# Key rows and row sums of the first sequence's v by 0/1 matrices on TensorE, loads in the order k and q, v, weights, and conversions of weight sets 2 to 4 queued behind attention unit 3

## The chip, the core and the metric

One Trainium2 chip, of which the kernel uses one core. The metric is the device time of one execution in microseconds (us): 1023.42 us, the median of three runs (1019.8 to 1023.69). Five engines run their own queues in order: TensorE (PE, with its weight loads as PEld), VectorE (DVE), ScalarE (ACT), GpSimd (POOL) and SyncE (SP), which issues all DMAs.

## The reference

The inputs q, k, v are 4 sequences x 8 heads x 576 rows x 64 channels, fp32. Two attentions are added, and two expert layers follow on the 2304 x 512 result:

```python
q_d = q.reshape(B, H, Sd, factor, D).mean(axis=3)     # factor 4: 144 rows; k_d, v_d alike
out_up = np.repeat(sm_attn(q_d, k_d, v_d), factor, axis=2)
mask = np.abs(pos[:, None] - pos[None, :]) < factor    # local attention, 7 keys a row
out = out_up + softmax(scale * q @ k.T where mask) @ v
x = ((g := x @ w_gate) * sigmoid(g) * (x @ w_val)) @ w_out       # 512 -> 1536 -> 512
h = x @ w_in;  x = (max(h, 0) + alpha * min(h, 0)) @ w2_out       # 512 -> 2048 -> 512
```

## The kernel before, in words

Attention goes in units: a unit `n` is two heads and half a sequence (288 rows), four units a half, so units 0 to 7 are the first sequence. A unit transposes q (and, in the first half, k) on TensorE (`a_T`), multiplies them (`a_QK`), takes the two softmaxes (`a_EXP`, `a_NRM`), transposes the weights of the coarse one (`a_PT`) and multiplies both with v (`a_PV`), whose result `xf` is split into a high and a low part, `xh` and `xl`.

`a_PV` needs v in two forms. `vw` holds the key rows in windows: for each 24 queries 32 rows of v, 128 partitions a tile. For it `stage(0)` copies v into a DRAM tensor `vwin` with overlapping windows, and `a_load_w` reads that back. `vs` holds sums of four neighbouring rows: `a_load_v` loads v once more as `vd`, and `a_vd` adds on GpSimd (L321, L322).

The expert layers multiply in three fp32r products of high and low parts. So every weight tile is converted once: `w_split` takes a raw tile through ScalarE (L126), VectorE (L127, L128), ScalarE (L131) and GpSimd (L132). A set j is three tiles, g, v and o, of the first layer (12 sets). The first layer runs over 8 blocks of 288 rows: block 0 is units 0 to 3, and its step j multiplies with tile g (`m_g`, ended by L502), tile v (`m_v`, ended by L508) and, one step later, tile o (`m_y`). During block 0 all 12 sets are loaded and converted. The later units run beside the matmuls.

SBUF is full: attention tiles of units 0 to 7 live in slots of weight tiles that come later (`pslot`). Of the 24 slots of sets 4 to 11, in the order g4 v4 o4 g5, v5 o5 g6 v6, o6 g7 v7 o7, g8 v8 o8 g9, v9 o9 g10 v10, the first four hold `qv` (q and vw of units 0 to 3), the next four `qs` (softmax tiles), then `kn`, `vd` and `bd`. Units 4 to 7 put their `qv` where `kn` was and their `qs` where `vd` was. A weight tile is loaded when the attention tile in its slot has been read for the last time. The converted halves go through three staging tiles in rotation (`st_slots`).

A scheduler orders each engine's queue by a time model of its own; `tc.issue_after` holds an instruction behind a named one. In `prep1` the table `gP` puts GpSimd's part of sets 1, 2 and 3 behind units 0 and 3, the other engines' parts are not held. The loads of unit 8 stand behind the load of tile o7.

Of the kernel before, what the change touches and what calls it, by code (L numbers as in the profile page):

```python
# [15 lines left out]
DRAM = bass.MemoryType.DRAM  # L16


K = dict(kdP=0, qdP=0, dnP=2, ldn=9, lo='asvw0123', NPRO=8, c=5, a1=1, a2=0, OFF=25, oT=3, oE=3, oP=5, oV=11, vd1=2, vd2=1, pre=(1, 1, 0, 0), lo1=0, lo2=1, nst=3, nrm=0, sub=0, nrm1=0, sub1=0, qtA=0, ldw=1, xl1=0, ly=4, l2=3, st2=2, early=1, w2p=1, la=0, bdV=0, sp=9, s2=0, s3=0, gj=7, gs=1, vr=0, kc=0, gD=(0, 0, 0, 0, 0, 0), gP=(0, 2, 8, 8, 0, 0), gA=(0, 0, 0, 0, 0, 0))


@with_exitstack
def attn_moe_moe2_kernel(
# [113 lines left out]
    pbd = {}  # L137
    kds = {}
    vss = {}
    vds = {}  # L140
    bds = [ap_.tile([128, 2, NW, 128], F32, name=f"bd{i}", bufs=1) for i in range(NBD)]

    def coords(n):
# [4 lines left out]
    order = [f"{kind}{j}" for j in range(F1 - 8, F1) for kind in "gvo"]  # L148
    st_slots = order[5 * NP:][:K["nst"]]
    NEARLY = F1 - 2  # L150
    pslot = {(what, n): order[4 * i + n] for i, what in enumerate(("qv", "qs", "kn", "vd", "bd")) for n in range(NP)}
    for n in range(NP):
        pslot["qv", n + NP] = pslot["kn", n]
        pslot["qs", n + NP] = pslot["qs" if K["vr"] else "vd", n]
    NPRO = K["NPRO"]
    srs = [ap_.tile([128, 8], F32, name=f"sr{i}", bufs=1) for i in range(4)]

    def at_(n, shape, tag):
        return wp.tile(shape, F32, tag=pslot[tag, n], name=tag)
# [23 lines left out]
    def a_load(n):  # L183
# [22 lines left out]
        for h in range(2):  # L206
            nc.sync.dma_start(out=qn[:, :, h], in_=q[b, h0 + h, t0:t0 + HB, :].rearrange("(r p) c -> p r c", p=QB))

    def a_load_v(n):
        b, half, hp, blk = coords(n)  # L210
        h0 = 2 * hp
        if half == 0:
            hu[n]["vd"] = []
            if n < NP:
                vd = vds[hp] = at_(n, [72, 2, 2, 4 * D], "vd")
                nc.sync.dma_start(out=vd.rearrange("p h f x -> p (h f) x"),
                                  in_=v[b, h0:h0 + 2].rearrange("h (f p r) c -> p (h f) (r c)", f=2, r=4))
            for f in range(2):
                if n < NP:
                    hu[n]["vd"].append(vd[:, :, f])  # L220
                    continue
                vf = ap_.tile([72, 2, 4 * D], F32, tag="vd", name="vd", bufs=NVD)
                hu[n]["vd"].append(vf)
                nc.sync.dma_start(out=vf, in_=v[b, h0:h0 + 2, f * HB:(f + 1) * HB].rearrange("h (p r) c -> p h (r c)", r=4))

    def a_load_w(n):

        b, half, hp, blk = coords(n)
        if n < NP:
            pbd[n] = at_(n, [128, 2, NW, 128], "bd")  # L230
            (nc.vector if K["bdV"] else nc.gpsimd).memset(pbd[n], 0.0)
        if n >= NPRO:
            hu[n]["vw"] = ap_.tile([128, NW, 2, D], F32, tag="vw", name="vw", bufs=NVW)
        t = hu[n]["vw"]
        for h in range(2):
            w0 = ((b * H + 2 * hp + h) * 2 + half) * NW * 128
            nc.sync.dma_start(out=t[:, :, h], in_=vwin[w0:w0 + NW * 128, :].rearrange("(w p) c -> p w c", p=128))

    def stage(b):

        nw = H * S // SUB
        g0, g1, ng = b * nw, (b + 1) * nw, B * nw

        def win(a, e):
            n = (e - a) * SWIN
            nc.sync.dma_start(
                out=vwin[a * SWIN:e * SWIN, :].rearrange("(g r) c -> g (r c)", r=SWIN),
                in_=bass.AP(v.tensor, v.offset + (a * SUB - 3) * D, [[SUB * D, e - a], [1, SWIN * D]]))

        vf = v.rearrange("b h s c -> (b h s) c")  # L250
        if g0 == 0:
            nc.sync.dma_start(out=vwin[0:3, :], in_=vf[0:3, :])
            nc.sync.dma_start(out=vwin[3:SWIN, :], in_=vf[0:SWIN - 3, :])
            win(1, 16)
            g0 = 16
# [56 lines left out]

    def a_vd(n):
        b, half, hp, blk = coords(n)
        if n < NPRO and K["vr"]:
            return
        if half == 0:
            vs = vss[hp] = ap_.tile([72, 2, 2, D], F32, tag=f"vs{hp}", name="vs", bufs=1)
            for f in range(2):
                vv = hu[n]["vd"][f].rearrange("p h (r c) -> p h r c", r=4)  # L320
                nc.gpsimd.tensor_tensor(out=vv[:, :, 0:2], in0=vv[:, :, 0:2], in1=vv[:, :, 2:4], op=ALU.add)  # L321
                nc.gpsimd.tensor_tensor(out=vs[:, f], in0=vv[:, :, 0], in1=vv[:, :, 1], op=ALU.add)  # L322

    def a_QK(n, A):
        b, half, hp, blk = coords(n)
# [94 lines left out]
    def a_PV(n, A):  # L420
        b, half, hp, blk = coords(n)
        d = hu[n]
        pt, vw, bd = d["pt"], d["vw"], d["bd"]
        if n < NPRO and K["vr"]:
            vd = vds[hp].rearrange("p h f (r c) -> p h f r c", r=4)
            for f in range(2):
                for r in range(4):
                    for h in range(2):
                        nc.tensor.matmul(A[64 * h:64 * h + 64, 1, 0:QD], vd[:, h, f, r], pt[:, h, f * QD:(f + 1) * QD],
                                         start=(f == r == 0), stop=(f == 1 and r == 3))  # L430
        else:
            vs = vss[hp]
            for f in range(2):
                for h in range(2):
                    nc.tensor.matmul(A[64 * h:64 * h + 64, 1, 0:QD], vs[:, f, h], pt[:, h, f * QD:(f + 1) * QD],
                                     start=(f == 0), stop=(f == 1))
# [12 lines left out]
        nc.gpsimd.tensor_sub(xl[:, hp], xf, f32(xh[:, hp]))
        del hu[n]  # L450
# [26 lines left out]
    def gate(n, stage):  # L477

        bb = tc.nc.cur_bb.bb.instructions
        for key, eng in (("D", nc.vector), ("P", nc.gpsimd), ("A", nc.scalar)):  # L480
            gates[key, n, stage] = next(i for i in reversed(bb) if i.engine == eng.engine)

    def prep1(j):
        with ExitStack() as es:
            for key in "DPA":
                g = K["g" + key][j] if j < 6 else 0
                if g and (key, (g - 1) // 2, (g - 1) % 2) in gates:
                    es.enter_context(tc.issue_after(gates[key, (g - 1) // 2, (g - 1) % 2]))
# [129 lines left out]

    if True:
        make_identity(nc, ident)  # L620
        for tok in K["lo"]:
            if tok == "s":
                stage(0)
            elif tok in "avw":
                for n in range(NP):
                    {"a": a_load, "v": a_load_v, "w": a_load_w}[tok](n)
            elif tok == "x":
                for n in range(NP):
                    a_load_v(n)
                    a_load_w(n)  # L630
            else:
                load1(int(tok))
# [20 lines left out]
        P = [ATT, Y[0], Y[1], pgv.tile([128, 2, 512], F32, name="gv")]  # L653
        def a_all(n, A):
            a_T(n, A)
            if K["vd1"] == 0:
                a_vd(n)
            a_QK(n, A)
            gate(n, 0)
            if K["vd1"] == 1:  # L660
                a_vd(n)
            a_EXP(n)
            a_NRM(n)
            gate(n, 1)
# [169 lines left out]
```

## Time and profile before

| what | value |
|---|---|
| median of three runs | 1023.42 us |
| profiled execution, its own time | 1022.0 us |
| its span, first to last instruction | 1020.1 us |
| PE busy | 970.3 us, 95% of the span |
| DVE, POOL, ACT busy | 496.7, 387.7, 292.3 us |
| PE idle in the first 51.73 us | 28.4 us |

The 1.9 us between the span and the profiled time lie around the program and are not touched by the change. In the 40 slices of the profile PE is under 90% busy only in the first six and in the last one, so the time of this kernel beyond its matmuls lies in the first 150 us. There DVE is the busiest engine (5898884 in its first seven slices), and the DMA engines are at eight to nine tenths in the first three.

### The profile page before, as it was taken

How to read it: one execution, taken by the hardware profiler on the slowest of the kernel's cores; microseconds unless marked ns; L12 is line 12 of the kernel's file. 1: busy time of each engine (PE TensorE's matmuls, PEld its weight loads, DVE VectorE, ACT ScalarE, POOL GpSimd, SP SyncE). 2: the span in 40 equal slices, each digit the busy share in tenths (PEclk: the TensorE clock that was granted, in tenths of full speed). 3: DMA queues.
4: the chain of work that ended last, by engine and by line, in shares of the span. 5: the costliest groups of instructions: out<-in, count | busy, mean ns of one | idle time of the engine just before them, and what ended most of it. 6: DMA issues, size and time to landing. Idle time of an engine off the chain costs nothing.

```text
span 1020.1 us, 19253 instructions
## 1 busy us (share of the span) xinstructions
PE 970.3 (95%) x7760; PEld 867.5 (85%) x7760; DVE 496.7 (49%) x1045; ACT 292.3 (29%) x660; POOL 387.7 (38%) x492
## 2 busy tenths in 40 slices
PE   5388789999999999999999999999999999999997
PEld 4288789999999999999999998888888888888896
DVE  5898884546453646353532769722322322322232
ACT  3656542222222222222223656312101101111111
POOL 5868773233422343322223335724223322322222
PEclk9999999999999999999999999999999999999999
DMA  8996751123120232110103884102000100100010
GB/s 199 289 305 217 196 139 39 35 67 60 42 51 16 54 71 45 38 29 15 43 13 88 290 265 127 42 1 62 21 0 19 55 1 1 42 11 0 1 43 21
DMA packets 135895, 77.81 MB, mean 76 GB/s; under 512 B 97407, under 2 KB 127103, under 8 KB 135039
## 3 DMA queue, kind: packets, MB, share of 16 engines
q1 hardware_dynamic: 135804, 76.58, 27.0%
q8 instruction: 60, 0.98, 0.4%
q14 instruction: 31, 0.25, 0.1%
HBM read 67.12 MB, written 15.73 MB: 81 GB/s over the span
## 4 chain that ended last, share of the span: by engine, by line
PE 79%; DVE 7%; DMA 6%; SPq 4%; issue 2%; POOL 2%; ACT 1%; DVEq 0%; POOLq 0%; ACTq 0%
PE y L599 6%; PE y L601 6%; PE y L600 6%; PE g L462 6%; PE v L463 6%; PE v L462 5%; PE g L464 5%; PE g L463 5%; PE v L464 5%; PE y L462 4%; PE y L464 4%; PE y L463 4%; PE h L462 3%; PE h L464 3%; PE h L463 3%
## 5 line engine op out<-in xcount | busy, mean ns | idle before, releaser
L587 POOL TENSOR_TENSOR gl<-t,gh 128x512 fp32r<-128x512 f32 (+1 forms) x80 | 97.0, 1214 | 250.6 <-ACT gh L586 244.1
L462 PE MATMUL g<-xh,w 128*128 128x288 f32 x384 | 117.0, 305 | 13.4 <-DVE u L502 8.8
L586 ACT CAST gh<-t 128x512 fp32r<-128x512 f32 (+1 forms) x80 | 46.1, 578 | 278.4 <-DVE t L583 239.0
L463 PE MATMUL y<-pl,w 128*128 128x288 f32 x384 | 114.3, 300 | 3.2 <-POOL pl L512 3.2
L462 PE MATMUL v<-xh,w 128*128 128x288 f32 x384 | 116.5, 303 | 0.0
L463 PE MATMUL v<-xl,w 128*128 128x288 f32 x384 | 116.0, 302 | 0.0
L464 PE MATMUL g<-xh,w 128*128 128x288 f32 x384 | 114.6, 298 | 1.2 <-POOL w L132 1.2
L464 PE MATMUL v<-xh,w 128*128 128x288 f32 x384 | 114.7, 299 | 0.0
L463 PE MATMUL g<-xl,w 128*128 128x288 f32 x384 | 114.6, 298 | 0.0
L599 PE MATMUL y<-w,gh 128*128 128x512 f32 x288 | 113.2, 393 | 1.0 <-ACT sy L531 1.0
L502 DVE SCALAR_TENSOR_TENSOR u<-u,g 128x288 f32<-128x288 f32 x96 | 43.3, 451 | 144.2 <-ACT u L501 144.1
L464 PE MATMUL y<-ph,w 128*128 128x288 f32 x384 | 113.5, 298 | 0.0
L600 PE MATMUL y<-w,gh 128*128 128x512 f32 x288 | 112.8, 392 | 0.0
L601 PE MATMUL y<-w,gl 128*128 128x512 f32 x288 | 112.0, 392 | 0.0
L462 PE MATMUL y<-ph,w 128*128 128x288 f32 x384 | 111.2, 303 | 0.3 <-ACT ph L511 0.3
L512 POOL TENSOR_TENSOR pl<-u,ph 128x288 fp32r<-128x288 f32 x96 | 80.8, 842 | 56.0 <-ACT ph L511 55.7
L132 POOL TENSOR_TENSOR w<-st,w 128x512 fp32r<-128x512 f32 x52 | 73.8, 1425 | 59.5 <-ACT w L131 57.8
L462 PEld LDWEIGHTS g<-xh,w 128*128 128x128 f32 x384 | 73.2, 191 | 16.8 <-DVE u L502 10.8
L581 DVE TENSOR_SCALAR t<-h,alpha 128x512 f32<-128x512 f32 (+1 forms) x40 | 27.9, 697 | 110.7 <-PE h L464 109.5
L463 PEld LDWEIGHTS y<-pl,w 128*128 128x128 f32 x384 | 72.4, 189 | 4.4 <-POOL pl L512 3.9
L462 PEld LDWEIGHTS y<-ph,w 128*128 128x128 f32 x384 | 71.0, 189 | 5.1 <-issue 4.2
L463 PEld LDWEIGHTS v<-xl,w 128*128 128x128 f32 x384 | 73.5, 191 | 1.7
(188 smaller groups left out, 2116.3 us busy)
## 6 DMA issues: line engine op xcount, KB each, us to landing
raw<-in_moe_w_out_dram SPq DMA_DIRECT2D x28, 512.0 KB, 4.5
raw<-in_moe_w_in_dram SPq DMA_DIRECT2D x16, 512.0 KB, 5.2
raw<-in_moe_w_gate_dram SPq DMA_DIRECT2D x12, 512.0 KB, 9.5
raw<-in_moe_w_val_dram SPq DMA_DIRECT2D x12, 512.0 KB, 8.7
vw<-vwin SPq DMA_DIRECT2D x48, 96.0 KB, 2.4
out_dram<-os SPq DMA_DIRECT2D x18, 256.0 KB, 2.5
sy<-y SPq DMA_DIRECT2D x16, 256.0 KB, 2.9
y<-ys SPq DMA_DIRECT2D x14, 288.0 KB, 2.9
```

What stands on the lines that cost most here:

```text
L132: eng.tensor_sub(w[:, 1], st, f32(w[:, 0]))
L462: nc.tensor.matmul(o, lhi, rhi, start=first, stop=False)
L463: nc.tensor.matmul(o, lhi, rlo, start=False, stop=False)
L464: nc.tensor.matmul(o, llo, rhi, start=False, stop=last)
L502: nc.vector.scalar_tensor_tensor(out=u, in0=u, scalar=1.0, in1=GV[0][:, :HB], op0=ALU.add, op1=ALU.mult)
L512: nc.gpsimd.tensor_sub(pl, u, f32(ph))
L581: nc.vector.tensor_scalar(out=t[:, :n], in0=P[:, :n], scalar1=0.0, scalar2=alpha_sb[:, j:j + 1], op0=ALU.min, op1=ALU.mult)
L586: nc.scalar.copy(out=gh[:, :n], in_=t[:, :n])
L587: nc.gpsimd.tensor_sub(gl[:, :n], t[:, :n], f32(gh[:, :n]))
L599: nc.tensor.matmul(o, gh[:, ms], ohi, start=(j == 0), stop=False)
L600: nc.tensor.matmul(o, gh[:, ms], olo, start=False, stop=False)
L601: nc.tensor.matmul(o, gl[:, ms], ohi, start=False, stop=(j == F2 - 1))
```

## The change

For the first sequence the DRAM copy, its read-back, the `vd` loads and GpSimd's adds go. In their place one tile `vn` a head pair (104 partitions, 6 x 96-row steps with 3 rows before and 5 behind, read from v) is multiplied with two 0/1 matrices that GpSimd makes at the start: `selw` gives all `vw` rows of a unit in one product of 384 columns, `sel4` the sums of four rows in six products of 128 columns, in the first half only. ScalarE copies both out of PSUM (`a_V`). `vn` takes the slots of `vd`, and must stay until unit n+4 has used it; so the `qs` of units 4 to 7 now take the slots of the `qs` of units 0 to 3. The load order becomes k and q, v, then sets 0 to 3. All engines' parts of set 1 are held behind unit 3's softmax, those of sets 2 and 3 behind unit 3's last instructions. (Sets are numbered from 0 here; the title's sets 2 to 4 are j = 1 to 3.)

```diff
+    VR = QB + 8
-        pslot["qs", n + NP] = pslot["qs" if K["vr"] else "vd", n]
+        pslot["qs", n + NP] = pslot["qs", n]
...
+    def a_load_n(hp):
+        vn = vns[hp] = at_(hp, [VR, S // QB, 2, D], "vn")
+        for h in range(2):
+            r0 = (2 * hp + h) * S - 3
+            a = max(0, -r0)
+            nc.sync.dma_start(out=vn[a:, :, h],
+                              in_=bass.AP(v.tensor, v.offset + (r0 + a) * D, [[D, VR - a], [QB * D, S // QB], [1, D]]))
...
+    def a_V(n, A):
+        b, half, hp, blk = coords(n)
+        vn = vns[hp].rearrange("p r h c -> p r (h c)")
+        nc.tensor.matmul(A[:, 0, 0:NW * 128], selw, vns[hp].rearrange("p r h c -> p (r h c)")[:, half * NW * 128:(half + 1) * NW * 128],
+                         start=True, stop=True)
+        nc.scalar.copy(out=hu[n]["vw"].rearrange("p w h c -> p (w h c)"), in_=A[:, 0, 0:NW * 128])
+        if half == 0:
+            for f in range(2):
+                for r in range(NW):
+                    nc.tensor.matmul(A[:72, 1, f * 128:(f + 1) * 128], sel4[:, r], vn[:, NW * f + r],
+                                     start=(r == 0), stop=(r == NW - 1))
+            vs = vss[hp] = ap_.tile([72, 2, 2, D], F32, tag=f"vs{hp}", name="vs", bufs=1)
+            nc.scalar.copy(out=vs.rearrange("p f h c -> p (f h c)"), in_=A[:72, 1, 0:256])
...
+    behind = {1: (NP - 1, 1), 2: (NP - 1, 2), 3: (NP - 1, 2)}
...
+            if j in behind:
+                for key in "DPA":
+                    es.enter_context(tc.issue_after(gates[(key, *behind[j])]))
...
-        for tok in K["lo"]:
-            if tok == "s":
-                stage(0)
...
+        for n in range(NP):
+            a_load(n)
+        for hp in range(NP):
+            a_load_n(hp)
+        for j in range(4):
+            load1(j)
...
         def a_all(n, A):
             a_T(n, A)
             a_QK(n, A)
             gate(n, 0)
-            if K["vd1"] == 1:
-                a_vd(n)
             a_EXP(n)
+            a_V(n, A)
             a_NRM(n)
```

The first place is PE's queue at the end of units 0 to 3. PSUM tiles att, y_69, y_70 and gv belong to units 0, 1, 2 and 3. Before:

```order
L338 MATMUL gv<-kd,qs 72x144 x2
L415 MATMUL y_69<-ident,qs 72x72 x4
L435 MATMUL att<-qs,vs 64x72 x4
L439 MATMUL att<-bd,qv 64x96
L435 MATMUL y_69<-qs,vs 64x72 x4
L439 MATMUL att<-bd,qv 64x96 x5
L439 MATMUL y_69<-bd,qv 64x96
L415 MATMUL y_70<-ident,qs 72x72 x2
L439 MATMUL y_69<-bd,qv 64x96 x5
```

Now:

```order
L331 MATMUL y_70<-vn,sel_82 72x128 x6
L427 MATMUL y_69<-ident,qs 72x72 x4
L439 MATMUL att<-qs,vs 64x72 x4
L443 MATMUL att<-bd,qv 64x96 x6
L325 MATMUL gv<-vn,selw 128x384
L427 MATMUL y_70<-ident,qs 72x72 x4
L439 MATMUL y_69<-qs,vs 64x72 x4
L443 MATMUL y_69<-bd,qv 64x96 x6
L331 MATMUL gv<-vn,sel_82 72x128 x6
```

The selector products of units 2 and 3 now stand between the last products of units 0 and 1; those of units 0 and 1 stand earlier, within the scores of units 2 and 3.

The second place is DVE's queue from unit 3's result (`gv`) to the first use of a block-0 product (u<-u,g). The `st` rows are weight conversions. Before:

```order
L444 TENSOR_TENSOR qs<-gv,qs 128x288
L128 SCALAR_TENSOR_TENSOR st_1009<-raw,st_1009 128x512
L127 TENSOR_SCALAR st_1009<-st_1009 128x512
L128 SCALAR_TENSOR_TENSOR st_1009<-raw,st_1009 128x512
L127 TENSOR_SCALAR st_1066<-st_1066 128x512
L128 SCALAR_TENSOR_TENSOR st_1066<-raw,st_1066 128x512
L127 TENSOR_SCALAR st_1066<-st_1066 128x512
L128 SCALAR_TENSOR_TENSOR st_1066<-raw,st_1066 128x512
L502 SCALAR_TENSOR_TENSOR u<-u,g 128x288
```

Now, its first rows (six conversions and twelve attention steps in all stand before the same u<-u,g, now L508):

```order
L448 TENSOR_TENSOR qs<-gv,qs 128x288
L310 TENSOR_REDUCE qs<-qs 128x72
L295 COPY qs<-y_69 128x288
L310 TENSOR_REDUCE qs<-qs 128x72
L127 TENSOR_SCALAR st_1021<-st_1021 128x512 x2
L128 SCALAR_TENSOR_TENSOR st_1021<-raw,st_1021 128x512 x2
L127 TENSOR_SCALAR st_1034<-st_1034 128x512 x2
L355 TENSOR_TENSOR qs<-att,mask 128x2x96
L356 TENSOR_REDUCE mx<-att 72x2
L295 COPY qs<-y_70 128x288
```

Twelve conversions stand before the first u<-u,g in both, half of them now behind unit 3, and with them the first steps of units 4 to 6.

The third place is SP's queue where unit 7 ends. raw_931 and raw_939 are tiles o7 and g9 of before:

```order
L103 DMA raw_931<-in_moe_w_out_dram 128x1024
L246 DMA vwin_64<-in_v_dram 192x2048
L195 DMA kn_946<-in_k_dram 32x18x32 x4
L195 DMA qn_951<-in_q_dram 32x9x32 x4
L105 DMA raw_939<-in_moe_w_gate_dram 128x4x256
```

Now raw_956 is o7 and raw_948 is v6:

```order
L103 DMA raw_956<-in_moe_w_out_dram 128x1024
L250 DMA vwin_64<-in_v_dram 192x2048
L198 DMA kn_971<-in_k_dram 32x18x32 x4
L198 DMA qn_976<-in_q_dram 32x9x32 x2
L105 DMA raw_948<-in_moe_w_val_dram 128x4x256
```

The tile that waits for unit 7's last reading is now v6 of set 6, where it was g9 of set 9.

## Rows read from the trace of the kernel before

**Rows 1.** Busy time of the engines in five stretches.
```profile
core 0: us, PE busy (x) PEld busy (x) DVE busy (x) ACT busy (x) POOL busy (x), PEclk, DMA share, GB/s
0.00:51.73 51.73, 23.37 (x341) 17.38 (x341) 34.69 (x86) 24.12 (x62) 35.54 (x71) 1.00 0.91 242
29.23:59.30 30.07, 14.81 (x108) 12.69 (x108) 29.37 (x48) 18.83 (x44) 24.49 (x27) 1.00 0.91 250
59.30:110.27 50.97, 46.90 (x562) 42.85 (x562) 46.74 (x98) 31.52 (x81) 35.63 (x41) 0.97 0.76 267
110.27:150.84 40.57, 32.83 (x314) 30.31 (x315) 35.35 (x73) 20.28 (x42) 32.52 (x35) 0.92 0.67 153
170.00:300.00 130.00, 129.93 (x1411) 123.74 (x1412) 66.50 (x175) 33.91 (x90) 44.38 (x79) 1.00 0.22 48
```

**Rows 2.** Timeline of PE: start, us, engine, line, operation, [idle before, releaser].
```profile
4.29 1.19 PE L283 MATMUL att<-ident,kn 96*128 96x96 f32 x6 [4.29 <-DMA kn<-in_k_dram]
35.86 1.06 PE L439 MATMUL att<-bd,qv 128*64 128x96 f32 x9 [5.49 <-DMA qv<-vwin]
46.89 1.23 PE L439 MATMUL gv<-bd,qv 128*64 128x96 f32 x12
51.73 0.61 PE L462 MATMUL g<-xh,w 128*128 128x288 f32 x1 [3.62 <-DVE qs L444]
57.17 0.44 PE L463 MATMUL v<-xl,w 128*128 128x288 f32 x1
57.41 0.44 PE L464 MATMUL v<-xh,w 128*128 128x288 f32 x1
...
103.78 0.67 PE L439 MATMUL att<-bd,qv 128*64 128x96 f32 x12
150.42 0.29 PE L463 MATMUL y<-pl,w 128*128 128x288 f32 x1
150.55 0.29 PE L464 MATMUL y<-ph,w 128*128 128x288 f32 x1
```

**Rows 3.** Timelines of POOL, ACT and DVE where they wait for v and weights.
```profile
20.70 1.41 POOL L321 TENSOR_TENSOR vd<-vd 72x256 f32<-72x256 f32 x2 [2.90 <-DMA vd<-in_v_dram]
28.21 0.51 POOL L360 TENSOR_TENSOR qs<-qs,mx 128x192 f32<-128x192 f32 x1
...
28.53 0.67 ACT L126 ACTIVATE st<-raw 128x512 f32<-128x512 f32 x1 [6.66 <-DMA raw<-in_moe_w_gate_dram]
29.23 1.06 DVE L127 TENSOR_SCALAR st<-st 128x512 int32<-128x512 int32 x1 [7.92 <-ACT st L126]
```

**Rows 4.** The same five engine columns, with DMA share and GB/s, in DMA-bound stretches.
```profile
0.00:28.50 28.50, 15.29 (x262) 11.22 (x262) 12.78 (x45) 8.34 (x24) 16.56 (x48) 1.00 0.88 215
...
0.00:10.00 10.00, 4.18 (x67) 3.29 (x67) 1.89 (x8) 1.92 (x2) 7.97 (x33) 1.00 0.80 166
60.00:90.00 30.00, 27.48 (x417) 24.77 (x417) 26.85 (x68) 18.30 (x55) 18.00 (x28) 0.98 1.04 364
```

**Rows 5.** Groups of DVE, 59.3 to 110.27 us: busy, mean ns, idle before.
```profile
L128 DVE SCALAR_TENSOR_TENSOR st<-raw,st 128x512 int32<-128x512 int32 x15 | 15.4, 1034 | 0.3
L127 DVE TENSOR_SCALAR st<-st 128x512 int32<-128x512 int32 x14 | 9.7, 699 | 1.5 <-ACT st L126 1.4
...
L311 DVE TENSOR_REDUCE qs<-qs 128x72 f32<-128x288 f32 x4 | 1.8, 449 | 0.1
```

**Rows 6.** Timeline of DVE: first use of block 0, and unit 7's result.
```profile
59.30 0.46 DVE L502 SCALAR_TENSOR_TENSOR u<-u,g 128x288 f32<-128x288 f32 x1
...
110.27 0.45 DVE L444 TENSOR_TENSOR qs<-att,qs 128x288 f32<-128x288 f32 x1
```

**Rows 7.** Where unit 7 ends: queue of SP, timeline of POOL, chain of waits.
```profile
113.89 0.39 SPq L105 DMA_DIRECT2D raw<-in_moe_w_gate_dram  x1
...
112.89 0.98 POOL L449 TENSOR_TENSOR xl<-qs,xh 128x288 fp32r<-128x288 f32 x1
...
114.33 4.03 DMA vd<-in_v_dram
```

More of the change, by code (lines that the diff above doesn't have):

```diff
@@ L16 @@
 DRAM = bass.MemoryType.DRAM
-K = dict(kdP=0, qdP=0, dnP=2, ldn=9, lo='asvw0123', NPRO=8, c=5, a1=1, a2=0, OFF=25, oT=3, oE=3, oP=5, oV=11, vd1=2, vd2=1, pre=(1, 1, 0, 0), lo1=0, lo2=1, nst=3, nrm=0, sub=0, nrm1=0, sub1=0, qtA=0, ldw=1, xl1=0, ly=4, l2=3, st2=2, early=1, w2p=1, la=0, bdV=0, sp=9, s2=0, s3=0, gj=7, gs=1, vr=0, kc=0, gD=(0, 0, 0, 0, 0, 0), gP=(0, 2, 8, 8, 0, 0), gA=(0, 0, 0, 0, 0, 0))
+K = dict(kdP=0, qdP=0, dnP=2, ldn=9, lo='asvw0123', NPRO=8, c=5, a1=1, a2=0, OFF=25, oT=3, oE=3, oP=5, oV=11, vd1=2, vd2=1, pre=(1, 1, 0, 0), lo1=0, lo2=1, nst=3, nrm=0, sub=0, nrm1=0, sub1=0, qtA=0, ldw=1, xl1=0, ly=4, l2=3, st2=2, early=1, w2p=1, la=0, bdV=0, sp=9, s2=0, s3=0, gj=7, gs=1, vr=0, kc=0)
 @with_exitstack
@@ L139, in attn_moe_moe2_kernel @@
     vss = {}
-    vds = {}
+    vns = {}
+    VR = QB + 8
     bds = [ap_.tile([128, 2, NW, 128], F32, name=f"bd{i}", bufs=1) for i in range(NBD)]
@@ L150, in attn_moe_moe2_kernel @@
     NEARLY = F1 - 2
-    pslot = {(what, n): order[4 * i + n] for i, what in enumerate(("qv", "qs", "kn", "vd", "bd")) for n in range(NP)}
+    pslot = {(what, n): order[4 * i + n] for i, what in enumerate(("qv", "qs", "kn", "vn", "bd")) for n in range(NP)}
     for n in range(NP):
         pslot["qv", n + NP] = pslot["kn", n]
-        pslot["qs", n + NP] = pslot["qs" if K["vr"] else "vd", n]
+        pslot["qs", n + NP] = pslot["qs", n]
     NPRO = K["NPRO"]
+    selw = ap_.tile([VR, 128], F32, name="selw", bufs=1)
+    sel4 = ap_.tile([VR, NW, 72], F32, name="sel4", bufs=1)
     srs = [ap_.tile([128, 8], F32, name=f"sr{i}", bufs=1) for i in range(4)]
@@ L207, in a_load @@
             nc.sync.dma_start(out=qn[:, :, h], in_=q[b, h0 + h, t0:t0 + HB, :].rearrange("(r p) c -> p r c", p=QB))
+    def a_load_n(hp):
[5 more added lines that the diff above has]
+                              in_=bass.AP(v.tensor, v.offset + (r0 + a) * D, [[D, VR - a], [QB * D, S // QB], [1, D]]))
+            if a:
+                nc.sync.dma_start(out=vn[:a, 1:, h],
+                                  in_=bass.AP(v.tensor, v.offset + (r0 + QB) * D, [[D, a], [QB * D, S // QB - 1], [1, D]]))
+                nc.sync.dma_start(out=vn[:a, 0, h], in_=bass.AP(v.tensor, v.offset, [[D, a], [1, D]]))
     def a_load_v(n):
@@ L213, in a_load_v @@
             hu[n]["vd"] = []
[L214 to L217, printed above, removed]
             for f in range(2):
-                if n < NP:
-                    hu[n]["vd"].append(vd[:, :, f])
-                    continue
                 vf = ap_.tile([72, 2, 4 * D], F32, tag="vd", name="vd", bufs=NVD)
@@ L228, in a_load_w @@
         b, half, hp, blk = coords(n)
[L229 to L234, printed above, removed]
+        t = hu[n]["vw"] = ap_.tile([128, NW, 2, D], F32, tag="vw", name="vw", bufs=NVW)
         for h in range(2):
@@ L250, in stage @@
         vf = v.rearrange("b h s c -> (b h s) c")
[L251 to L255, printed above, removed]
         if g1 == ng:
@@ L314, in a_vd @@
         b, half, hp, blk = coords(n)
-        if n < NPRO and K["vr"]:
-            return
         if half == 0:
@@ L423, in a_PV @@
         pt, vw, bd = d["pt"], d["vw"], d["bd"]
[L424 to L436, printed above, removed]
+        vs = vss[hp]
+        for f in range(2):
+            for h in range(2):
+                nc.tensor.matmul(A[64 * h:64 * h + 64, 1, 0:QD], vs[:, f, h], pt[:, h, f * QD:(f + 1) * QD],
+                                 start=(f == 0), stop=(f == 1))
         for w in range(NW):
@@ L481, in gate @@
             gates[key, n, stage] = next(i for i in reversed(bb) if i.engine == eng.engine)
+    behind = {1: (NP - 1, 1), 2: (NP - 1, 2), 3: (NP - 1, 2)}
     def prep1(j):
         with ExitStack() as es:
[L485 to L488, printed above, removed]
+            if j in behind:
+                for key in "DPA":
+                    es.enter_context(tc.issue_after(gates[(key, *behind[j])]))
             prep1_(j)
@@ L620, in attn_moe_moe2_kernel @@
         make_identity(nc, ident)
-        for tok in K["lo"]:
-            if tok == "s":
-                stage(0)
[L624 to L632, printed above, removed]
+        for n in range(NP):
[4 more added lines that the diff above has]
+            load1(j)
+        for n in range(NP):
+            pbd[n] = at_(n, [128, 2, NW, 128], "bd")
+            nc.gpsimd.memset(pbd[n], 0.0)
+        nc.gpsimd.memset(selw, 0.0)
+        nc.gpsimd.affine_select(out=selw.rearrange("p (i r) -> p i r", i=NS), in_=selw.rearrange("p (i r) -> p i r", i=NS),
+                                pattern=[[-SUB, NS], [-1, SWIN]], compare_op=ALU.not_equal, fill=1.0, base=0, channel_multiplier=1)
+        nc.gpsimd.memset(sel4, 1.0)
+        nc.gpsimd.affine_select(out=sel4, in_=sel4, pattern=[[QB, NW], [-4, 72]], compare_op=ALU.is_ge, fill=0.0,
+                                base=-3, channel_multiplier=1)
+        nc.gpsimd.affine_select(out=sel4, in_=sel4, pattern=[[-QB, NW], [4, 72]], compare_op=ALU.is_ge, fill=0.0,
+                                base=6, channel_multiplier=-1)
+        nc.gpsimd.affine_select(out=sel4, in_=sel4, pattern=[[-24, NW], [1, 72]], compare_op=ALU.is_ge, fill=0.0,
+                                base=0, channel_multiplier=0)
+        nc.gpsimd.affine_select(out=sel4, in_=sel4, pattern=[[24, NW], [-1, 72]], compare_op=ALU.is_ge, fill=0.0,
+                                base=23, channel_multiplier=0)
         for t in srs:
@@ L655, in a_all @@
             a_T(n, A)
-            if K["vd1"] == 0:
-                a_vd(n)
             a_QK(n, A)
             gate(n, 0)
-            if K["vd1"] == 1:
-                a_vd(n)
             a_EXP(n)
+            a_V(n, A)
             a_NRM(n)
             gate(n, 1)
-            if K["vd1"] == 2:
-                a_vd(n)
             a_PT(n, A)
-            if K["vd1"] == 3:
-                a_vd(n)
             a_PV(n, A)
+            gate(n, 2)
         pc = [0]
@@ L688, in attn_moe_moe2_kernel @@
             a_load(n)
-            a_load_w(n)
         for n in range(NP, NPRO):
```

## The prediction

> **What bounds the kernel now.** I read first the busy time by stretch, then the timelines of the engines where they wait, then the groups of VectorE. From 170 us on TensorE is full: 129.93 of 130.00 us [rows 1]. No work is added there, so the change can only move the moment at which that full stretch begins. I mark it by the last product of block 0, which starts at 150.55 and lasts 0.29, so it ends at 150.84 [rows 2].
>
> Before that mark TensorE is busy 23.37 of 51.73 us, and then never full [rows 1]. Its first waits come from v: 5.49 us for the read-back of the windows, then 3.62 us for unit 3's result on VectorE, after which block 0 starts at 51.73 [rows 2]. GpSimd waits for the second copy of v until 20.70, and the softmax step of unit 2 (L360), which needs none of it, stands behind those additions until 28.21 [rows 3]. The first weight tile is awaited by ScalarE until 28.53; VectorE starts converting at 29.23 after 7.92 us idle [rows 3]. From there VectorE is the limit: 29.37 busy of 30.07 us up to the first use of a block-0 product at 59.30, then 46.74 of 50.97 up to unit 7's result at 110.27 [rows 1, 6]. In the last 40.57 us before the mark it is 35.35 and TensorE 32.83, neither is full, and the two wait for each other [rows 1].
>
> **The change, step by step.**
>
> Loads. Removed are 1.57 MB of window copy, 1.57 MB of read-back and 1.18 MB of `vd`; added are eight `vn` loads of 104 x 6 x 64 words, 1.28 MB. Up to 28.50 us the DMA engines moved 28.5 x 215 = 6.13 MB [rows 4]. Ahead of the first weight tile now stand k and the first half of q (1.18 and 0.59 MB, as before) and the 1.28 MB of v, all in rows of 256 B as k and q are. These ran at 166 GB/s and 0.80 busy, 207 when full [rows 4]: 3.05 MB take 14.7 us. With some 1.5 us of start and 2.1 us for the tile (0.52 MB at 215/0.88 = 244 GB/s) it lands between 18.5 and 20; I take 20.0, and 20.7 for VectorE, 8.5 us earlier than 29.23. Here a rule of the Trainium skill speaks against the change: its page DMA: Bandwidth & Descriptors, Specifications, wants 512 B or more a transfer for line rate, and the removed window copy had 8 KB, the new rows 256 B. The trace agrees: 207 GB/s against 364 at 1.04, 350 when full, later [rows 4]. If 256 B cost nothing, the v rows would take 3.7 us instead of 6.2 and the tile would land 2.5 us earlier still; the sum goes by the slow rate.
>
> Products on TensorE. `selw` has 384 columns and `sel4` six times 128, and an fp32 product is two records, so 768 and 1536 columns a unit. Their price is not in the trace. From below: 12 records of 96 columns in 0.67 us with the clock at the faster pace [rows 2], 0.58 ns a column, 0.45 and 0.89 us. From above: six transposes of 96 columns in 1.19 us [rows 2], 2.07 ns, 1.59 and 3.17 us. In this part of the program the 12 records take 1.23 us [rows 2], so the slow pace holds, and two heads share the array there, which this product cannot; I take 1.30 and 2.56, near the upper end. Units 0 to 3 then cost 15.4 us (5.4 to 19.0), inside 28.4 us of idle time [rows 1]. Units 4 to 7 cost four `selw` products at half of it, 2.6 us (1.8 to 6.4), in a stretch where TensorE has 4.1 us idle [rows 1]. Following the queue, the last `sel4` leads to unit 3's result at about 39.6 (all at the lower prices) to 43.8 us (as taken), where block 0 waited for it until 51.73 [rows 2]. VectorE has by then six conversions and the steps of the units to do, some 22 us from 20.7, so at 43 it is no earlier itself. I charge no wait; without that cover it is 0 to 4 us.
>
> VectorE to the first use of block 0. Before 30.07 us. Added in front of the same instruction are unit 3's score steps (three of the same kind, 1.1 us) and those of units 4 to 6 (4.2 us: the twelve attention steps of the second order place, of which the longest kind takes 0.45 [rows 5], at 0.35 on average). The additions of GpSimd that ran beside the first conversions are gone: the first L127 took 1.06 us against a mean of 0.70 later [rows 3, 5]; for the four conversions there I give 1.5 us (0 to 3). So 30.07 + 5.3 - 1.5 = 33.9, and 20.7 + 33.9 = 54.6 instead of 59.30.
>
> To unit 7's result. Before 50.97 us. The 4.2 us are done already, and the new order has 13 conversions in this stretch instead of 14 L127 and 15 L128, 0.70 + 2 x 1.03 = 2.8 us less [rows 5]. So 44.0, and 98.6 instead of 110.27: 11.7 us earlier. ScalarE's copies (eight of 384, four of 256 columns, by the 0.4 to 0.6 us of its copies some 5 us) lie in idle time, ScalarE being busy 31.52 of 50.97 [rows 1].
>
> From there to the mark. This is what the change costs. Tile v6 now lies under unit 7's softmax tile, and can be loaded only when unit 7's `xl` is done. Before, g9 had this place: `xl` at 112.89 to 113.87, its load issued at 113.89, and the DMA behind it landed 4.03 us after 114.33 [rows 7]; it was needed three sets later. For v6: result to `xl` 3.6 us (110.27 to 113.87), landing 4.1, then conversion through ScalarE, VectorE and ScalarE with what is queued there, 4.3: products with v6 start 12.0 us after unit 7's result. Tiles g8 and v8 share a staging tile with v6, so they follow 4.0 us after the v6 products. After that TensorE has 216 products of 288 columns in all (72 v, 48 g, 72 y of block 0, 24 of block 1), 0.13 us each [rows 2], 28.8 us with the weight loads, and 2.8 us of units 8 and 9. So 12.0 + 4.0 + 31.6 = 47.6 instead of 40.57: 7.0 us later (bounds 0, if other products fill the wait, to 12, if v6 meets the full queue of the copy for the next sequence).
>
> Sum: the mark moves by -11.7 + 7.0 = -4.7, from 150.84 to 146.2. The profiled execution took 1022.0 us, 1.4 under the median of the three runs, which I leave as noise: 1022.0 - 4.7 = 1017.3.
>
> The wait for v6 brings the clock in. Products stand 0.24 us apart from 51.73 on, after an idle time, and 0.13 at 150.42 [rows 2]: the two levels, 1.2 and 2.4 GHz. The Trainium skill, TensorE: Matmul & The Clock Gate, on HAM oscillation, says that idle gaps bring the lower level back; the rows agree. Three microseconds at the lower level would cost 1.5, which I leave in the range.
>
> **The rivals.**
>
> First, the wait for v6 is covered. TensorE idles 7.7 us in the 40.57 already [rows 1]; if the new wait only takes that place, all 11.7 us stay: 1010.3. For it: the new order puts the y products of steps 4 and 5 and g of 6 and 7 between, 48 products, 6.4 us. Against it: 12 us from result to v6 is longer than that.
>
> Second, slower, by one mechanism: the slot of v6. If unit 7 ends no earlier than now, the 7.0 us stand alone: 1029.0. It decides at a result of unit 7 later than 150.84 - 47.6 = 103.2 us. For it: the conversions of sets 2 and 3 now all stand before the first use of block 0, and unit 7 is queued behind them. Against it: VectorE is full and starts 8.5 us sooner.
>
> Third, nothing changes: unit 3 comes late because the selector products cost the upper price (19.0 instead of 15.4) on the path, so that 4 of the 4.7 us go: 1021.
>
> **How the numbers follow.** Forecast 0.42, own range 1013 to 1021; covered wait 0.26; no change 0.18; slower 0.14. I count 0.5%, 5.1 us, as what a measurement can tell: faster means under 1018.3, slower over 1028.5. Of the forecast six tenths lie under 1018.3, with the covered wait 0.51 faster; the rest and the third rival give 0.35 for no change; the second 0.14. The range of 1009 to 1026 leaves out most of the second rival and a little below the first.
>
> **What would show it.** In the changed profile: ScalarE's first L126 near 20 us; no wait of TensorE for `qv`; unit 3's result near 40 to 44; the first use of block 0 near 55; unit 7's result near 99; then a wait of TensorE of several microseconds at a v product, ended by v6's conversion, and the end of block 0 near 146. A first conversion after 25 us, or unit 7 after 103, would make it wrong on one side; v products that never wait after unit 7, on the other.

## The result, and the profile after

The changed kernel takes 1036.26 us (median of 4 runs, 1034.75 to 1038.52) against 1023.29 for the kernel before beside it: ratio 1.0136, 95% interval 1.0109 to 1.0163, so 13 to 14 us slower where 1017.3 was predicted. The profiled execution took 1037.7 us with a span of 1035.8.

First the busy time by stretch (columns as in [rows 1, 4]: length, busy time of PE, PEld, DVE, ACT and POOL, granted clock, DMA share, GB/s). The first three stretches run from VectorE's first conversion to the first use of block 0, on to unit 7's result, and on to the end of block 0.

```profile
29.07:67.86 38.79, 33.76 (x352) 26.44 (x351) 30.93 (x65) 24.03 (x61) 21.36 (x27) 0.95 0.95 299
67.86:111.11 43.25, 38.09 (x342) 34.62 (x343) 38.78 (x80) 29.12 (x78) 31.00 (x33) 0.89 0.60 192
111.11:166.06 54.95, 46.53 (x379) 42.91 (x377) 39.47 (x72) 21.74 (x44) 34.80 (x42) 0.78 0.51 123
170.00:300.00 130.00, 130.00 (x1413) 123.88 (x1412) 66.93 (x176) 32.37 (x88) 43.84 (x80) 1.00 0.22 46
```

From 170 us on TensorE is full as before, so the loss is the moment at which that begins: block 0 ends at 166.06 instead of 150.84. VectorE, full before its first use of block 0 [rows 1], is now busy 30.93 of 38.79 us there. And the last stretch has 54.95 us instead of 40.57 [rows 1], with a mean granted clock of 0.78.

The start, in SyncE's queue (start, duration, line; a duration reaches to where the queue goes on):

```profile
9.18 0.36 SPq L218 DMA_DIRECT2D vn<-in_v_dram  x1
9.58 8.54 SPq L221 DMA_DIRECT2D vn<-in_v_dram  x1
18.16 0.28 SPq L223 DMA_DIRECT2D vn<-in_v_dram  x1
18.48 4.56 SPq L218 DMA_DIRECT2D vn<-in_v_dram  x7
23.09 0.83 SPq L105 DMA_DIRECT2D raw<-in_moe_w_gate_dram  x1
```

The first row is the load of the first head's v. It begins before the tensor does, so it was cut to 101 of 104 rows, and the three left come by L221 and L223. That small L221 stands 8.54 us. Seven loads of 104 rows then pass in 4.56 us. What came of it (PE, ACT, then DVE; in brackets the idle time before and what ended it):

```profile
21.46 1.62 PE L325 MATMUL att<-vn,selw 104*128 104x384 f32 x2 [5.85 <-DMA vn<-in_v_dram]
...
26.26 2.83 PE L331 MATMUL att<-vn,sel 104*72 104x128 f32 x12
...
28.38 0.66 ACT L126 ACTIVATE st<-raw 128x512 f32<-128x512 f32 x1 [4.78 <-DMA raw<-in_moe_w_gate_dram]
...
29.07 0.43 DVE L127 TENSOR_SCALAR st<-st 128x512 int32<-128x512 int32 x1 [3.83 <-ACT st L126]
...
53.55 0.45 DVE L448 TENSOR_TENSOR qs<-gv,qs 128x288 f32<-128x288 f32 x1
...
67.86 0.43 DVE L508 SCALAR_TENSOR_TENSOR u<-u,g 128x288 f32<-128x288 f32 x1
```

The first conversion is where it was [rows 3], not 8.5 us earlier; unit 3's result (L448) and the first use of block 0 (L508) come 2.3 and 8.6 us later than before [rows 6]. Unit 3's result before:

```profile
51.23 0.45 DVE L444 TENSOR_TENSOR qs<-gv,qs 128x288 f32<-128x288 f32 x1
```

Then the place behind unit 7's result, on DVE, SP, ACT and PE:

```profile
111.11 0.46 DVE L448 TENSOR_TENSOR qs<-att,qs 128x288 f32<-128x288 f32 x1 [0.51 <-ACT qs L447]
...
106.72 5.97 SPq L198 DMA_DIRECT2D kn<-in_k_dram  x4
112.73 2.86 SPq L198 DMA_DIRECT2D qn<-in_q_dram  x2
115.69 0.40 SPq L105 DMA_DIRECT2D raw<-in_moe_w_val_dram  x1
...
125.73 0.62 ACT L131 CAST w<-st 128x512 fp32r<-128x512 f32 x1 [1.66 <-DVE st L128]
...
119.03 0.29 PE L468 MATMUL g<-xh,w 128*128 128x288 f32 x1
123.27 0.76 PE L346 MATMUL att<-kT,qT 64*32 64x32 f32 x48 [3.95 <-DVE qT L279]
...
126.40 0.61 PE L466 MATMUL v<-xh,w 128*128 128x288 f32 x1 [1.69 <-ACT w L131]
```

Tile v6 is loaded at 115.69, behind the k and q loads of the next sequence, and its first product starts at 126.40. Between 119.3 and that, TensorE has only attention work. It waits twice there: 3.95 us for a transposed q of the next sequence (`qT`, L279), then 1.69 us for v6's conversion. So the slot of v6 is a theory up to this point; e3 tests it.

### The profile page after: what moved, and what is told of

Same layout as the page of the kernel before. It is cut to its first block, busy times and chain, and to the rows that moved or that the text cites. A ratio compares the mean times of both kernels' runs of the same rounds, so it can differ in the third digit from the quotient of the medians.

```text
span 1035.8 us, 19371 instructions
## 1 busy us (share of the span) xinstructions
PE 996.9 (96%) x7824; PEld 887.4 (86%) x7824; DVE 495.3 (48%) x1045; ACT 296.4 (29%) x672; POOL 375.0 (36%) x483
## 4 chain that ended last, share of the span: by engine, by line
PE 82%; DVE 6%; DMA 4%; SPq 3%; issue 2%; ACT 1%; POOL 1%; DVEq 0%; ACTq 0%; POOLq 0%
PE y L605 6%; PE y L607 6%; PE y L606 6%; PE g L466 6%; PE v L467 6%; PE v L466 6%; PE g L468 6%; PE g L467 6%; PE v L468 5%; PE y L466 4%; PE y L468 4%; PE y L467 4%; PE h L466 3%; PE h L468 3%; PE h L467 3%; DVE st L128 2%
## 5 line engine op out<-in xcount | busy, mean ns | idle before, releaser
L466 PE MATMUL g<-xh,w 128*128 128x288 f32 x384 | 118.6, 309 | 7.8 <-DVE u L508 7.8
L468 PE MATMUL g<-xh,w 128*128 128x288 f32 x384 | 116.2, 303 | 1.6 <-POOL w L132 1.6
L467 PE MATMUL g<-xl,w 128*128 128x288 f32 x384 | 117.6, 306 | 0.0
L508 DVE SCALAR_TENSOR_TENSOR u<-u,g 128x288 f32<-128x288 f32 x96 | 43.4, 452 | 148.3 <-ACT u L507 148.3
L466 PEld LDWEIGHTS g<-xh,w 128*128 128x128 f32 x384 | 74.7, 195 | 10.3 <-DVE u L508 9.2
L468 PEld LDWEIGHTS g<-xh,w 128*128 128x128 f32 x384 | 75.0, 195 | 2.5 <-POOL w L132 1.9
L467 PEld LDWEIGHTS g<-xl,w 128*128 128x128 f32 x384 | 74.9, 195 | 1.1 <-issue 1.0
L466 PEld LDWEIGHTS v<-xh,w 128*128 128x128 f32 x384 | 73.7, 192 | 2.6 <-ACT w L131 2.1
```

The lines of the kernel that those rows point to most:

```text
L466: nc.tensor.matmul(o, lhi, rhi, start=first, stop=False)
L467: nc.tensor.matmul(o, lhi, rlo, start=False, stop=False)
L468: nc.tensor.matmul(o, llo, rhi, start=False, stop=last)
L508: nc.vector.scalar_tensor_tensor(out=u, in0=u, scalar=1.0, in1=GV[0][:, :HB], op0=ALU.add, op1=ALU.mult)
```

## The experiments

Theories. A: two separate costs, the 101-row load ahead of unit 7 and the slot of v6 behind it. Rivals: a SyncE queue that was merely full, the price of the selector products on TensorE, and the hold on the conversions. Ratios are to the kernel before on the same chip, with 95% intervals.

**e1: the first v load in 96 and 5 rows.**

```diff
-    dma_start(out=vn[a:, :, h], ...)                      # a = 3 for the first head: 101 rows
+    for p0, p1 in ((a, VR),) if a == 0 else ((a, a + QB), (a + QB, VR)):
+        dma_start(out=vn[p0:p1, :, h], ...)               # 96 and 5 rows
```

> The changed kernel with its first v load (101 rows of 6 x 64 words) cut into 96 and 5 rows; all else alike. Theory A (the 101 rows went through one DMA engine at 18 GB/s, and SyncE stood 8.5 us behind them): no SyncE row of 8 us, the first w_gate load is issued near 14.5 us instead of 23.1, TensorE does not wait 5.9 us for vn, the first L126 starts near 20 instead of 28.4, unit 3's result comes at 47 to 48 instead of 53.6, unit 7's at 103 to 106 instead of 111.1; the end of block 0 moves by as much, and the time is 1028 to 1031 us. Rival B (SyncE was held by a full queue behind k and q, whatever the shape of the load): the same stall of 6 to 9 us, first w_gate near 23, time 1034 to 1038. Rival C (the stall goes, but the front is set by TensorE's selector products and by the held conversions): first L126 near 20, unit 7's result still at 109 or later, time 1033 to 1037.

Measured: 1028.76 us, ratio 1.0045 (1.0028 to 1.0062). The stall is gone and the events move by 6.2 to 8.6 us (SP, ACT, DVE):

```profile
10.81 6.08 SPq L219 DMA_DIRECT2D vn<-in_v_dram  x7
16.93 0.80 SPq L105 DMA_DIRECT2D raw<-in_moe_w_gate_dram  x1
...
21.47 0.67 ACT L126 ACTIVATE st<-raw 128x512 f32<-128x512 f32 x1 [1.52 <-DMA raw<-in_moe_w_gate_dram]
...
45.76 0.44 DVE L449 TENSOR_TENSOR qs<-gv,qs 128x288 f32<-128x288 f32 x1
...
60.70 0.43 DVE L509 SCALAR_TENSOR_TENSOR u<-u,g 128x288 f32<-128x288 f32 x1
...
102.52 0.46 DVE L449 TENSOR_TENSOR qs<-att,qs 128x288 f32<-128x288 f32 x1 [0.51 <-ACT qs L448]
```

Unit 7's result comes 8.6 us earlier, and block 0 ends 8.3 us earlier, at 157.74: the stretch between the two stays, 55.2 us. Theory A's first half holds, and its time; the first weight load came 2.4 us later than it said, the results of units 3 and 7 1.2 and 0.5 us ahead of its ranges. Rivals B and C fall.

**e8: other row counts.** Base is the kernel with both edits (e4, below); six of the eight loads are cut.

```diff
+    c = {0: 99, 2: 103, 3: 102, 4: 100, 5: 98, 6: 97}.get(2 * hp + h, VR)    # where head h of pair hp is cut
+    for p0, p1 in ((a, c), (c, VR)) if c < VR else ((a, VR),):
```

> The kernel with both edits, in which six of the eight v loads are cut into a large and a small part, large parts of 96, 103, 102, 100, 98 and 97 rows (two stay at 104 rows). Theory R1 (a load is spread over as many DMA engines, up to 16, as divide its rows): SyncE stands 8 to 9 us behind the 103 rows and again behind the 97, 1 to 3 us behind the 102 (6 engines), and not behind 100 and 98 (10 and 14 engines); first w_gate 16 to 19 us later than 16.5, time 1032 to 1040. Theory R2 (rows not a multiple of 8 go through one engine): five stalls of 8 us, first w_gate after 50 us, time over 1050. Rival R3 (only the place, the first v load of the program, counts): no stall, 1020 to 1023.

Measured once: 1035.08 us. SyncE's queue behind the 103 and behind the 97 rows, and what all queues moved between 10 and 34 us (GB/s in 40 slices of 0.6 us):

```profile
11.59 8.38 SPq L221 DMA_DIRECT2D vn<-in_v_dram  x1
...
20.02 3.23 SPq L221 DMA_DIRECT2D vn<-in_v_dram  x6
...
23.59 7.84 SPq L221 DMA_DIRECT2D vn<-in_v_dram  x1
...
GB/s 169 210 41 202 68 41 18 18 18 18 18 18 18 18 18 18 18 20 47 107 112 146 172 201 73 18 18 18 18 18 18 18 18 18 18 18 30 106 244 274
```

And a stretch within the first stall (columns as in the result, the last but one the mean busy share of the 16 DMA engines):

```profile
14.00:19.50 5.50, 4.66 (x85) 2.36 (x85) 4.98 (x17) 3.65 (x15) 1.48 (x3) 1.00 0.08 18
```

Two stalls, each with a plateau of 18 GB/s, and the DMA engines at a share of 0.08, little over one of 16; the six issues of the 102, 100 and 98 rows with their remainders pass in 3.23 us. 97, 101 and 103 have no divisor from 2 to 16; 102, 100 and 98 have 6, 10 and 14. Of R1 the two long stalls and the time hold; the first weight load came 15.3 us later than in e4, not 16 to 19, and what the 102 rows alone cost isn't seen. R2 and R3 fall. The Trainium skill, DMA: Bandwidth & Descriptors, Why a DMA increments its semaphore by 16 and not by 1, states this rule: a DMA runs on the largest number of engines up to 16 that divides the slowest dimension of both sides. The runs agree. They don't single it out: the counts that stalled are all odd and the other large ones all even, and no large count that is odd but has a divisor up to 16, such as 99, was run. By R1 one engine carried the 151.5 KB of the 101 rows (101 x 6 x 256 bytes), in 8.5 us: 18 GB/s.

**e3: slots unit by unit.** What lives until unit 4's result lies under v5, o5, g6, v6, and only unit 7's tiles under v9 to v10; before the edit unit 7 held v6, o7, g9 and v10.

```diff
-    pslot = {(what, n): order[4 * i + n] for i, what in enumerate(("qv", "qs", "kn", "vn", "bd")) for n in range(NP)}
+    pslot = {(what, n): order[4 * (n + 1) + i] for i, what in enumerate(("qs", "kn", "vn", "bd")) for n in range(NP)}
+    pslot.update({("qv", n): order[n] for n in range(NP)})
```

> The changed kernel with the slots laid out unit by unit: what lives until unit 4's result lies under v5 to v6, unit 5's under o6 to o7, unit 6's under g8 to g9, and only unit 7's under v9 to v10 (before the edit each group of four slots held the four units, and v6 waited for unit 7). The front of the program stays as it is. Theory A (v6's wait for unit 7, 15.3 us from the result to its first product, with TensorE falling to the lower level, makes up the 13.7 us that the stretch from unit 7's result to the end of block 0 is longer than before): v6 is loaded near 85 us, no wait of TensorE for v6, that stretch is 41 to 46 us instead of 54.3, time 1024 to 1029. Rival (VectorE's conversions and the copies for the next sequence set that stretch): it stays 50 us or more, time 1033 to 1037.

Measured: 1027.34 us, ratio 1.0031 (1.002 to 1.0042). Unit 7's result stays, at 111.35; the stretch to the end of block 0:

```profile
111.35:155.92 44.57, 40.43 (x370) 36.57 (x371) 38.38 (x68) 19.95 (x42) 33.91 (x36) 0.96 0.41 102
```

44.57 us instead of 54.95: 4.3 us less idle time of TensorE (4.1 instead of 8.4) and 6.1 us less busy time for nearly the same count of records, since fewer products stand at the lower level (granted clock 0.96, not 0.78; by the timelines some 20 of 242 products take 0.40 us or more, instead of some 60 of 249). The v tiles of sets 5 to 8 are loaded between 71.74 and 92.78, ahead of unit 7's result, and no wait of TensorE for a converted tile is left. Theory A's second half holds. It moves all four tiles that unit 7 held, so what v6 alone is worth was not separated.

**e4: both edits.**

> Both edits of the two kernels named e1 and e3: the first v load cut into 96 and 5 rows, and the slots laid out unit by unit. Theory A (two separate costs, of which the first acts before unit 7's result and the second behind it): the gains add, 1016 to 1021 us, faster than the kernel before or equal to it. Rival (they share one bound, VectorE's conversions): only the larger of the two gains shows, 1024 to 1029.

Measured: 1021.05 us, ratio 0.9976 (0.9963 to 0.9988), and in the repeat below 0.9978. Both gains show: 1.36% over before became 0.24% under it, against 0.91 and 1.05 points of the edits alone. The sum of the two would be 1.96 points, and 1.60 were measured.

**e4b: the same again.**

> The kernel with both edits (first v load cut, slots unit by unit) once more, beside the others: 1019 to 1022 us, 0.1 to 0.4% under the kernel before. If it comes out at 1023 or more, the first measurement was a lucky one and the two edits do no more than take back the loss.

Measured: 1020.70 us, 0.9978 (0.9966 to 0.999). So this version beats both kernels, the faster of them by 2 us.

**e2: the changed kernel without the hold on VectorE and ScalarE.**

```diff
-    behind = {1: (NP - 1, 1), 2: (NP - 1, 2), 3: (NP - 1, 2)}      # on "DPA"
+    behind = {1: (0, 1), 2: (NP - 1, 1), 3: (NP - 1, 1)}           # on "P"
```

> The changed kernel with the hold on the conversions as in the kernel before: only GpSimd's subtractions of sets 2, 3 and 4 queue behind units 0 and 3, ScalarE and VectorE are free to convert. Theory A: VectorE fills the 5 us it idles between 40 and 50 us and starts set 2 near 40; the first use of block 0 comes 3 to 6 us earlier than 67.9, unit 7's result 2 to 5 us earlier than 111.1, but v6 still waits for unit 7, so the time is 1031 to 1035. Rival (the hold costs nothing, since VectorE has the same work before unit 7 in either order): 1035 to 1038.

Measured: 1033.07 us, 1.0086 (1.0071 to 1.0102): 5 us by the ratios. Time and unit 7's result (106.70) are as theory A said, the way there isn't: unit 3's result comes at 62.62 and the first use of block 0 at 72.83, both later. The mark doesn't hold the gain either: block 0 ends at 165.34, only 0.7 us earlier, and the rest lies in products of later blocks (TensorE has 1474 records behind it at 180 us, 1441 in the changed kernel).

**e5: both edits and that one.**

> The kernel with both edits (first v load cut, slots unit by unit) and, on top, the hold on the conversions as in the kernel before (only GpSimd's subtractions queue behind units 0 and 3). In the kernel with both edits VectorE is busy 4.94 of 10 us between 30 and 40 and 6.99 between 40 and 50. Theory A (the hold costs what it cost without the edits, 3 us): VectorE over 9 in both stretches, unit 3's result later than 47.1, unit 7's 2 to 5 us earlier than 106.5, time 1016.5 to 1019.5. Rival (what VectorE does early it does not do late, and the later unit 3 holds up block 0): 1020 to 1024.

Measured: 1027.0 us, 1.0037 (1.0022 to 1.0052), worse than with the hold. Both expectations miss. VectorE fills its idle time as forecast (the kernel with both edits, then this one):

```profile
30.00:40.00 10.00, 10.00 (x72) 8.38 (x70) 4.94 (x15) 5.73 (x19) 3.07 (x5) 1.00 1.01 276
```

```profile
30.00:40.00 10.00, 9.06 (x85) 7.38 (x83) 9.10 (x22) 7.80 (x22) 7.12 (x7) 1.00 1.06 286
```

Unit 7's result comes at 99.70, earlier than in either execution of its base (106.52, and 102.22 in the repeat), but the stretch from there to the end of block 0 grows from 44.4 (both) to 53.0 us.

**e9: both edits, only set 2 free.** `behind = {2: (NP - 1, 2), 3: (NP - 1, 2)}`.

> The kernel with both edits, in which set 2 (the conversions of g1, v1, o1) is not held, sets 3 and 4 as in the changed kernel. VectorE has some 8 us idle between 30 and 50 us there, and in the kernel without any hold (e5) unit 3's result came 8 us later than with it. Theory A (a third of the held work fills the idle time without pushing unit 3): VectorE over 8 of 10 us from 30 to 40, unit 3's result 47 to 50, unit 7's 2 to 4 us earlier than 106.5, time 2 to 4 us below the repeat of the kernel with both edits. Rival (any conversion in front of unit 3 holds up block 0 by as much as it does ahead): within 1.5 us of the repeat.

Measured: 1025.82 us, 1.0026 (1.0011 to 1.0041), 0.5% over the repeat. Unit 3 came at 47.94 as expected, but VectorE was busy 7.35 us from 30 to 40, not over 8, and unit 7 came at 108.47, later than in either execution of its base. Both expectations miss.

**e10: the kernel before with the hold alone.** `gD`, `gP`, `gA` all `(0, 8, 8, 8, 0, 0)`.

> The kernel before with the hold alone: all conversions of sets 2, 3 and 4 on the three engines queue behind the first steps of unit 3's softmax, the rest as it was. Theory A (the hold empties VectorE between 30 and 50 us and is by itself a loss where unit 3 is late anyway): VectorE under 7 of 10 us in one of these stretches, first use of block 0 later than 59.3, time 1026 to 1033. Rival (the hold lets unit 3 end sooner and pays itself, as it did in the kernel with both edits): unit 3's result 2 us or more before 51.2, time 1018 to 1024.

Measured: 1030.93 us, 1.0082 (1.0066 to 1.0099). The time is theory A's. VectorE emptied less than it said (8.84 and 8.41 of 10 us, not under 7); the first use came at 62.54 instead of 59.30. So the hold costs 8 us in the kernel before and 5 in the changed one, and is worth 6 with both edits.

**e6: one of six `sel4` products.** `for r in range(1)` in place of `range(NW)` in that loop.

> The kernel with both edits, in which one of the six sel4 products of each group is left (5 of 6 left out, so the row sums of v are not those of the reference): 40 products less, some 9.4 us of TensorE at the 2.83 us that six of them took. Theory P (TensorE, full from 20 to 40 us, sets unit 3's result and by that the time): unit 3's result at 38 to 42 instead of 47.1, end of block 0 3 to 7 us earlier than 150.2, time 1014 to 1018. Rival (VectorE's conversions set the end of block 0): unit 3 as early, but the time within 1.5 us of 1021.

Measured: 1023.59 us, 1.0009 (0.9993 to 1.0024). Unit 3's result at 45.43 lies between those of the two executions of its base (47.14 and 42.70), and the time is no lower: theory P falls. TensorE isn't full any more (19.19 of 23.29 us from VectorE's first conversion to unit 3's result). By the ratios the time is 3 us above the base (0.9976 and 0.9978), so the rival's 1.5 us misses too. The order of TensorE's queue also changed, and no run takes the products away in the same order; in this kernel, fewer of them don't make it faster.

**e7: the kernel before with slots unit by unit.**

```diff
+    pslot = {(what, n): order[8 + 3 * n + i] for i, what in enumerate(("vd", "kn", "bd")) for n in range(NP)}
+    pslot.update({(what, n): order[4 * i + n] for i, what in enumerate(("qv", "qs")) for n in range(NP)})
```

> The kernel before with its slots laid out unit by unit: unit 4's three tiles under o6 to v7, unit 5's under o7 to v8, unit 6's under o8 to o9, unit 7's under v9... to v10's neighbours (before the edit o7, g9 and v10 waited for unit 7 together). It tells whether the layout alone speeds a kernel in which v6 never waited. Theory A (only the tile needed first after unit 7 counts, there o7, and it has some 25 us until it is used): 1022 to 1025. Rival (any wait for unit 7 costs): 1016 to 1020, and then the change itself is still a loss beside it.

Measured: 1024.04 us, 1.0009 (0.9992 to 1.0025). So the layout paid where v6 waited (e3), and not here, where o7, g9 and v10 did.

## Why the prediction was wrong, step by step

Its end of block 0 was 146.2 us; it came at 166.06, 19.9 us later. Its own terms add up to that: 8.4 for the start of the conversions, 4.9 up to the first use of block 0, -0.7 up to unit 7's result, 7.3 from there. With 1017.3 this makes 1037.2, where the profiled execution took 1037.7.

**Loads: the step that failed first.** "3.05 MB take 14.7 us" put one rate, 207 GB/s, on all rows of 256 B. The 0.15 MB of the 101-row load ran at 18, and SyncE's queue stood behind it, so VectorE began at 29.07 instead of 20.7. With that load cut it began at 22.17, so the rest of the step was 1.5 us short. The rate was read from loads of 96 rows and handed to one with another row count. Of the page DMA: Bandwidth & Descriptors of the Trainium skill the prediction weighed the rule on transfers under 512 B; the one on row counts, cited under e8, stands on the same page and bears on this load.

**Products on TensorE.** The prices were 1.65 and 2.83 us, not 1.30 and 2.56: 17.9 us for four units. "I charge no wait" failed: TensorE was all but full from 21.5 us on and gave unit 3's result at 53.55, in e1 at 45.76 (predicted 43.8). In the kernel with both edits, e6 took most of the `sel4` products away at no gain in time. What their price costs in the changed kernel itself, no run shows.

**VectorE to the first use of block 0.** 33.9 us were predicted and 38.8 came, 38.5 in e1. The work was not more, 30.93 us busy; the prediction kept VectorE full, though three sets were held until unit 3 and unit 3 hung on TensorE. It had counted the hold as a new order only, not as idle time:

```profile
40.00:50.00 10.00, 10.00 (x82) 7.98 (x80) 4.86 (x14) 4.79 (x15) 1.41 (x3) 1.00 0.95 205
```

But taking the hold off didn't shorten this step: in e2 VectorE was busy 9.28 and 9.10 us of 10 from 30 to 50, and the first use of block 0 came at 72.83 instead of 67.86. The 5 us that it gave back came behind this step. So the idle time is shown, and what would bring this step to 33.9 us isn't.

**To unit 7's result.** 44.0 us predicted, 43.25 measured: right.

**From there to the mark: the second failed step.** The mechanism, v6 under unit 7's tile, was right by e3; the 7.0 us were 14.4. Products with v6 start 15.3 us after unit 7's result instead of 12.0: the load waited for SyncE until 115.69, 2.3 us after `xl` was done at 113.39, and ScalarE took up its next tiles only at 122.78, 7.1 us behind the issue, not 4.1. And from 126.40 on 39.7 us were needed instead of 35.6, mostly because the products stood 0.24 us apart, the level of 1.2 GHz, until 139; the sum had priced them at 0.13, and 36 products at 0.11 us more are some 4 us. They stood 0.24 us apart from 111.60 to 118 as well, ahead of the wait for v6 and behind one of 2.70 us for VectorE, so not all of the lower level comes from v6. "Three microseconds at the lower level would cost 1.5" left that out of the sum. e3 takes back 10.4 of the 14.4 us. What is left, 44.6 against 40.57, is TensorE's: 370 of its records lie in that stretch instead of 314, so less was done ahead of unit 7's result.

**The rivals.** The second named the mechanism that won, and its point, unit 7 later than 103.2, was passed; its price, 1029.0, was short by the same 7.3 us. The first is refuted, since the wait was not covered. In the third the selector products cost 17.9 us, below its 19.0, and unit 3 came late as it says, but the time lies 15 us above its 1021. "A first conversion after 25 us, or unit 7 after 103, would make it wrong on one side": both came.

Open is why the hold changes sign between kernels. In e5 and e10 unit 7's result came earlier (by 2.5 to 6.8, and by 2.3 us) and the stretch behind it was longer (by 8.6 and 11.7). The scheduler had ordered every queue anew in both, and no run here holds the order fixed.

## What to carry to other kernels

Give a load a partition count that many DMA engines divide, and look at the odd first or last piece: cutting 101 rows into 96 and 5 was worth 9 us here. When a tile waits for the last user of its slot, price the wait with the issuing queue in front of it and with TensorE at the lower level behind it, and lay slots out so that the last unit holds the tiles that are needed last. Engine time that a hold leaves idle is a term of the sum, but measure the hold: it cost 8 and 5 us in two of these kernels and was worth 6 in the third.

## What the hardware showed that was not expected

One load of 101, 103 or 97 rows stopped the issue of all later DMAs of SyncE's queue for about 8 us each, while all 16 DMA engines together moved 18 GB/s at a mean busy share of 0.08 (e8).

TensorE's change of level is not fixed by the program. Two executions of the kernel with both edits, the first profile and the repeat, had the same instructions and, up to 32 us, the same times within 0.2 us:

```profile
30.16 2.76 PE L333 MATMUL y<-vn,sel 104*72 104x128 f32 x12
...
33.87 1.18 PE L445 MATMUL att<-bd,qv 128*64 128x96 f32 x12
...
38.67 2.83 PE L333 MATMUL gv<-vn,sel 104*72 104x128 f32 x12
...
44.81 1.18 PE L445 MATMUL gv<-bd,qv 128*64 128x96 f32 x12
```

```profile
30.05 2.76 PE L333 MATMUL y<-vn,sel 104*72 104x128 f32 x12
...
33.29 0.67 PE L445 MATMUL att<-bd,qv 128*64 128x96 f32 x12
...
35.88 1.53 PE L333 MATMUL gv<-vn,sel 104*72 104x128 f32 x12
...
39.96 0.67 PE L445 MATMUL gv<-bd,qv 128*64 128x96 f32 x12
```

TensorE had been busy almost without a break since 15.5 us in both. In the repeat the same products take half the time from 33 us on, the level of 2.4 GHz; in the other not before 45. The repeat's span is 4.3 us shorter (1015.4 against 1019.7). The granted clock of the rows by stretch doesn't show it: it is 1.00 from 30 to 40 us in both. So a moment read from one profile of these kernels can be 4 us off; the times are medians.
